# A fused cross-attention, Fourier mixing and MLP kernel: another order of the calls of its opening

## The chip, the cores and the metric

The kernel runs on one core of a Trainium2 chip. The metric is the device time of one execution in microseconds; a kernel's time is the median of several executions. Five engines work side by side, each through its own instructions in order: PE (TensorE, matrix products and transposes), DVE (VectorE), ACT (ScalarE), POOL (GpSimd) and SP (SyncE, which here only issues transfers). PE's results go into PSUM, a small memory in banks, from which DVE and ACT fetch them. Transfers to and from DRAM are issued by SP, ACT and POOL and are carried out by 16 DMA engines. Engines wait for each other by semaphores.

## The reference

For each of 8 batches there are two attentions, of the tokens `x` over the state and of the state over the tokens. Both results are set one below the other (512 + 32 = 544 rows of 8 heads x 64 = 512 columns). On this the real part of a two-dimensional Fourier transform is added, the rows are normed, and a two-layer perceptron is added.

```python
# x (8, 8, 512, 64), state (8, 8, 32, 64), float32
a = softmax(x @ state.T / 8);   xread = a @ state
a2 = softmax(state @ x.T / 8);  sread = a2 @ x
x = concatenate([xread, sread], axis=2)        # to (8, 544, 512)
u = x + real(fft(fft(x, axis=1), axis=2))
un = (u - mean(u)) / sqrt(var(u) + 1e-6)       # over the last axis
out = u + relu(un @ w_ch1) @ w_ch2             # 512 -> 2048 -> 512
```

## The kernel before

**How it is staged.** The batches run through a pipeline: while the perceptron of batch b keeps PE busy (`layer1`: products `ph`, ACT's `hT`; `layer2`: `po`, `poA`, `poB`), the attention of batch b+2 and the transform of batch b+1 are woven in. Tokens and state are cast to bf16 (`xin`, `stb`), transposed (`xT`, `sT`), multiplied to scores (`esp`), passed through the exponential on ACT, and multiplied by the state (`xrp`). DVE divides by the sums and writes the reads forwards and backwards as `XF` and `XR`. The transform along the 544 rows uses sums and differences of mirrored rows and columns (`Sm`, `SS`), multiplied by cosines and sines `TC`, `TS` and their negatives `NN` into `gp`; it is copied to `G` and multiplied by the second axis's table `TEO` into `yp`. `U` is the sum with x, `ub` its centred bf16 form, `tp` the transpose of `ub` on PE and `unT` its copy for `layer1`.

**The opening.** Before the first `ph` (at 22.4 us) nothing of the pipeline is full. `load_x(0)` fetches batch 0's tokens in seven pieces (four of 96 or 128 rows, then 15, 15 and 2 rows), two through ACT's queue and the rest through SP's, with `load_state(0, 1)` first on SP. `load_state(1, 2)` and `load_x(1)` do so for batch 1, all on SP. `turn_in_dram` copies a state mirrored from DRAM to DRAM (`s_dram`), and a later `load_state(..., s_dram)` reads it back into `gen`. `state_blocks(lo, hi, copy)` makes four casts into `stb`, one for each 32 partitions; batch 0's are ACT's, later ones POOL's. `cast_x` casts one piece of x to `xin`: for batch 0 one on ACT and three on DVE, for batch 1 on POOL. The sine tables come from counts: POOL's `iota` writes, DVE's `turn_steps` and `low_arguments` reduce them to angles in `gen`, and POOL's four `tensor_scalar` on `gi` make the second axis's angles. ACT evaluates them with its sine table and must load a table when it goes between sine and exponential; tiny activations on `gate2` (rows `gate` in the profile) stand where the load is to happen. `first_weights(lo, hi)` and `second_weights` issue the quarters of `w1` and `w2` on POOL, 512 KB each. `open_batch` holds batch 0's attention (`turn`, `score`, `read`, `sread`, `state_rows`, `even`, `odd`). `make_mirror` sets up `mirror` by a memset and an affine select on POOL; PE's `eTp` of batch 1 uses it. `warm(n)` issues n small products of `blank` whose results nobody uses.

**What sets the order.** All calls on the engines go through a `Recorder`, which stores them as 1748 numbered groups: one call each, except that consecutive products into the same PSUM bank, and batch 0's first loads, form one. At the end `play()` makes the calls in the order of the list `ORDER`. The text after it keeps that order on each engine; the waits between engines are derived from the data. So one call ahead of another of its engine in `ORDER` is ahead of it on the chip, and a call that waits holds up all that stand behind it on its engine. [...] `BANKS["psB"]` gives the bank, one digit for each tile of the pool `psB` in order of request; a tile waits for its bank's previous tile to be read out.

Because of the recorder every row in the profile carries line 63, where the stored call is made; rows are told apart by tile names and shapes. In the file, `ORDER` stands at line 68, `BANKS` at 133, `load_state` at 256, `load_x` at 265, `state_blocks` at 311, `low_arguments` at 404, `first_weights` at 459, `open_batch` at 718 and `warm` at 1269. The recorder's play and the gate that opens the sine table read:

```python
    def play(self):
        order = ORDER or range(len(self.groups))
        for n in order:
            for call in self.groups[n][1]:
                made = call()
...
    nc.vector.memset(gate2, 0.0)
    nc.scalar.activation(gate2[:, 1:2], gate2[:, 0:1], AF.Sin)
    state_ones(0, 2)
    state_blocks(0, 1)
    cast_x(0, nc.scalar.copy, 2, 3)
```

Of the kernel before, what the change touches and what calls it, by code (L numbers as in the profile page):

```python
# [49 lines left out]
class _Engine:  # L50
# [3 lines left out]
    def __getattr__(self, what):  # L54
# [14 lines left out]
        19 62 66 61 9-10 12 1 7 11 2 5 4 3 163 8 49 13 6 298 14 55 15 17 16 50 22 0 75-82 29 143 25 27 26 47 28 38 31 41 23  # L69
        144-145 40 39 32 146-147 30 20 46 21 42 48 148 43-45 149 18 24 34-35 33 37 36 72-74 83-118 130 119 329 120-121 123 122  # L70
        155 131 157 124 156 168 330 172 125 141 170 126 169 171 173 142 176 127-129 133-134 184 178 180 192 68 54 159 69-71 177
        185 193 59-60 58 67 64 316 63 65 187 189 186 135-137 188 138 194 196 195 197 139-140 153-154 216 174 331-332 175 206-210
        212 179 211 181 221 219 213 222 132 150-151 182 152 190 198-199 191 217 214 218 200 263 160 167 201-202 51 265 161
        203-204 267-268 165-166 205 299 162 56 261-262 300 158 264 304 266 297 307 303 302 301 57 228 232 229 220 225-227 224
        233 245 223 244 241 183 215 236-240 252-254 231 235 234 230 276-277 247-248 278-279 246 250-251 259 257 255 269 256 272
        249 242-243 258 271 274 284 270 273 317 312 310 309 319 315 314 313 311 318 280-283 285 290 292-293 291 294 275 286 288
        323 322 287 327 326 320 289 321 328 343 324 341 325 345 339 347 340 348 355 333 337 353 378 351 335 386 354 352 346 387
        361 360 342 338 344 385 379 362-365 367 308 260 366 368 52 296 358 382 381 398 356 390-391 380 383-384 521 392-393 396
        394 439 401 400 399 336 357 359 397 334 402-404 406 405 408 407 409 522 413-414 505 523-524 410 415 412 411 441 525 305
        371 370 369 373 422 374 419 375 426 424 420 423 53 526 421 417-418 459 457 349 376 455 453 461 476 465 388 463 473 469  # L80
        467 460 395 350 440 462 456 454 377 458 464 470 468 466 389 472 488 474 480 518 451 481 445-446 449 482 450 487 484 491
        442 492 447 485 496 475 477-478 443 448 495 500-501 506 429-430 428 427 452 591 493 486 479 483 529 536 497 516 498 489
        517 502 499 490 578 164 306 579 507 503 574 527 504 471 508 372 576 580 528 575 416 577 433 432 435 437 434 431 436 543
        582 512 532 519 530 494 583 514 444 520 531 550 533 539 537 589 509 540 538 560-563 510 555 544 556 545 511 438 546 549
        772 547 553 548 559 552 557 554 584 558 598 592 534 585-586 630 622 600 564 569 567 601 606 614 587-588 593 602-603 573
        568 572 570-571 607-608 596 595 597 594 609-610 621 611 613 612 616-617 625 618 627 626 620 619 604 541 624 632 637 599
        535 551 631 615 605 590 623 638 542 652 677 633 641 639 635 565 634 642 640 636 646 661 668 628 566 653 662 678 647 649
        671 654 648 655 670 663 669 664 684 689 685 690 680 682 650 644 659 672 629 683 658 681 667 651 688 693 645 673 660
        714-715 751 704 736-737 757 761 716-717 701 656 700 740 699 295 698 718 728 727 729 657 730 733 732 731 581 674-675
        694-695 679 767 762 782 708 774-775 768 922 745 744 705 771 742 769 741 746 743 738 752 739 754 756 706 763-764 758 755  # L90
        753 776-777 709 778 783 779-780 791 786 790 794-795 787 789 788 702-703 676 713 796 697 765 818 812 864 784 792 802 797
        804 816 814 871 759 808 719 820 766 813 865 819 793 803 785 798 815 805 817 760 809 821 830 823 711 725 720 710 825 726
        712 707 722 806 810 873 799 828 734 880 837 723 721 826 824 827 735 800 781 801 747-748 849 862 842 831 872 807 874 829
        881 836 835 846 850 838 840 839 841 811 863 845 843 852 870 724 773 770 851 750 844 866 858 856 875 911 832 893 877 884
        882 892 833 883 876 857 696 853 859 867 887-888 919 904 886 902 907 974 908 889-890 912 903 921 665-666 891 822 896 691
        847 895 848 899 898 897 900-901 692 686 643 687 954 932 914 878 909-910 920 894 955 928-929 934 968 834 960 957 959 925
        923-924 879 1102 941-942 970 980 996 963 917 976 905 1035 991 987 939 969 975 997 1046 981 933 906 1036 964 918 992 940
        930 913 931 935 943 916 915 937 944-948 938 971 965 949 966 986 950 977 988 967 953 952 951 978 984 993 1103 927 936 958
        973 926 962 961 956 1047 989 982 1007 985 994 979 990 983 1008 1048 1003 998 1012 1040 1009 1053 1022 1024 1058 1101
        1000 999 1001 1014 1005 1013 1004 1002 1041 1006 1054 1010 1025 1011 1060 1086 1061 1051 1067 1077-1078 1049 1062  # L100
        1015-1016 1063 1023 1059 1018 1027 1052 1064 1070 868 1071 1073-1074 1072 860 869 861 854 1075-1076 855 1079-1080 1050
        1087 1140 1017 1026 1031 1042 1280 1105 1104 1107 515 1134 1139 1137-1138 1106 1082 1037 1097-1098 1055 1119 1146 1084
        1236 1112 1069 1065 1056 1083 1099-1100 1066 1088 1038 1091 1113 1132 1108 1148 1094 1213 1166 1164 1110 1120 1019 1028
        1147 1237 1133 1114 1089-1090 1115-1116 1118 1117 1126 1122 1095 1081 1121 1124 1123 1141 1096 1143 1142 1130 1125 1111
        1144 1158 1205 1154 1092 1193 1162 1168 1127 1160 1149 1032 1085 1214 1165 1043 1109 1159 1167 1155 1206 1093 1194 1169
        1145 1131 1128 1161 1163 1174 1231 1207 1188 1219 1150 1175-1177 1151 1178 1057 1039 1136 1135 513 1179 1232 1220
        1181-1182 1180 1279 995 1020-1021 425 1029 1238-1239 1183 1172 1225 1156 1264 1191 1229 1226 1157 1192 1230 1185 1208
        1173 1171 1186 1189 1240 1184 1241 1190 1187 1243 1201 1196 1224 1197 1281-1282 1129 1068 1153 1200 1285 1195 1283-1284
        1209 1215 1255 1245 1256 1260 1227 1288 1257-1258 1244 1228 1247 1274 1261 1198 1030 1242 1044 1248 1250 1254 1249 1170
        1253 1199 1045 1033-1034 1275-1276 1221 1233 1335 1272 1277 1222 1289 1259 1265 1304 1273 1278 1308 1268 1305 1270  # L110
        1290-1291 1315 1252 1251 1267 1316 1292 1266 1234 1286 1321 1331 1297 1364 1343 1319 1327 1337 1376 1310 1407 1262 1293
        1269 1294 1296 1306 1295 1322 1312 1314 1332 1344 1299 1313 1300 1303 1301 1309 1342 1361 1302 1271 1202 1210 1287 1336
        1298 1320 1328 1216 1377 1365 1395 1408 1311 1338 1333 1325 1339 1359 1329 1340 1334 1326 1330 1317 1354 1402 1390 1360
        1318 1391 1403 1263 1398 1378 1435 1409-1410 1345 1357 1356 1355 1358 1379 1411 1399 1412 1348 1346-1347 1349 1367 1372
        1352 1368 1353 1307 1323 1235 1223 1386 1380 1366 1371 1413 1419 1421 1211-1212 1420 1217 1424-1425 1203-1204 1218 1341
        1423 1422 1369-1370 1392 1404 1426-1427 1416 1400 1362 1446-1447 1396 1384 1350 1428 1436 1429 1440 1393 1405 1363 1373
        1397 1351 1385 1401 1454-1455 1481 1491 1431 1441 1474 1461 1536 1450 1492 1482 1475 1462 1451 1439 1438 1418 1448-1449
        1456-1457 1468 1437 1458 1460 1459 1463 1476 1478 1464 1414-1415 1432 1445 1465-1466 1452 1512 1570 1499 1501 1489 1443
        1453 1477 1467 1444 1430 1497 1493 1469 1479 1537 1442 1513 1500 1490 1502 1498 1494 1472 1470 1473 1480 1516 1483 1507
        1495 1485 1524 1563 1519 1517-1518 1496 1520 1486 1508 1510 1509 1504 1511 1394 1406 1521 1505 1433 1538 1484 1527 1381  # L120
        1532 1525 1514 1564 1387 1528 1434 1515 1506 1523 1539 1522 1544 1554 1567 1558 1556 1550 1557 1540 1546 1471 1526 1531
# [1433 lines left out]
```

## Time and profile before

| what | value |
|---|---|
| time, median of three runs | 287.75 us (287.4 to 288.25) |
| profiled execution, its own time | 287.47 us |
| its span, from first to last instruction | 285.7 us |
| mean granted clock of PE | 0.997 |
| instructions | 6835 |
| PE busy in 0 to 10 us / 10 to 20 / 20 to 30 | 7.02 / 9.95 / 9.53 us |
| first product of `layer1` (`ph`) | 22.39 us |
| DMA engines' mean busy share of the span, first and second slice of 7.14 us | over 80%, over 90% |

The profiled execution's time is 1.77 us longer than its span: the span leaves out what lies around the instructions. In rows of the timeline the columns are start, duration, engine, line, operation, tiles, shapes and number of instructions, and in brackets the idle time of the engine before them with what ended it. `x4` after a row means that four instructions follow each other in it. Of a chain the columns are start, duration and what it consisted of. The page's slices:

```profile
PE   7899999999999999999999999999999999999993
DVE  6877777468899988985798688959766578224892
ACT  7897656746936576368377564586566653254000
POOL 8392476670660033502712119006200028000000
DMA  8999959966366346861379640413201520978366
```

Each digit is a tenth of a slice's time for which the engine was busy. PE is below nine tenths in the first two slices and the last one only.

### The profile page before, as it was taken

The page shows a single profiled execution, that of the slowest core. Times are in us where ns is not written, and L with a number is a line of the kernel's source. Part 1 is how long each engine was busy: PE and PEld are TensorE (multiplying, and loading weights), DVE is VectorE, ACT ScalarE, POOL GpSimd, SP SyncE. Part 2 cuts the span into 40 slices and gives each one's busy share as a digit, 9 for nine tenths or more (in the row PEclk, how much of TensorE's full clock was granted, in tenths as well). Part 3 has the DMA queues.
Part 4 walks back from the last instruction along what each step waited for, and adds up shares of the span by engine and source line. Part 5 has one row for each costly group of instructions (what it writes and reads, how often), then busy time and mean ns, then how long its engine had stood idle before and what let it go on. Part 6 is the DMA issues. An engine that isn't in the chain of part 4 may idle for free.

```text
span 285.7 us, 6835 instructions
## 1 busy us (share of the span) xinstructions
PE 275.2 (96%) x2615; PEld 199.0 (70%) x2644; DVE 210.6 (74%) x554; ACT 162.0 (57%) x327; POOL 92.5 (32%) x227
## 2 busy tenths in 40 slices
PE   7899999999999999999999999999999999999993
PEld 6788985555655778567758777576577667686882
DVE  6877777468899988985798688959766578224892
ACT  7897656746936576368377564586566653254000
POOL 8392476670660033502712119006200028000000
PEclk9999999999999999999999999999999999999998
DMA  8999959966366346861379640413201520978366
GB/s 156 185 181 190 202 95 181 197 146 153 83 157 103 93 116 156 107 170 25 80 169 194 149 94 19 98 53 65 84 0 48 151 65 18 182 149 136 92 162 184
DMA packets 110972, 34.91 MB, mean 122 GB/s; under 512 B 101996, under 2 KB 106476, under 8 KB 110940
## 3 DMA queue, kind: packets, MB, share of 16 engines
q1 hardware_dynamic: 100220, 28.72, 47.5%
q0 software_dynamic: 4224, 4.19, 9.7%
q10 hardware_dynamic: 6496, 1.57, 2.6%
q8 instruction: 20, 0.33, 0.5%
q14 instruction: 12, 0.10, 0.1%
HBM read 22.41 MB, written 14.02 MB: 128 GB/s over the span
## 4 chain that ended last, share of the span: by engine, by line
PE 87%; DVE 7%; DMA 2%; issue 1%; ACT 1%; SPq 1%; DVEq 0%
PE ph L63 39%; PE poA L63 18%; PE poB L63 13%; PE gp L63 4%; PE po L63 3%; PE yp L63 2%; DVE U L63 2%; DMA xs<-in_x_dram 2%; PE esp L63 2%; PE eTp L63 1%; PE xrp L63 1%; DVE XR L63 1%; PE xfp L63 1%; DVE ot L63 1%; SPq L63 1%
## 5 line engine op out<-in xcount | busy, mean ns | idle before, releaser
L63 PE MATMUL ph<-unT,w 128*128 128x512 bf16 (+2 forms) x743 | 127.9, 315 | 1.4
L63 ACT ACTIVATE hT<-ph 128x512 bf16<-128x512 f32 x128 | 72.1, 596 | 76.6 <-PE ph L63 76.3
L63 PEld LDWEIGHTS <-w 128*128 128x128 bf16 x768 | 64.3, 98 | 42.5 <-issue 0.6
L63 PEld LDWEIGHTS <-hT 128*128 128x128 bf16 x632 | 60.4, 98 | 14.8 <-issue 0.3
L63 DVE SCALAR_TENSOR_TENSOR ot<-poA,rstd,U 128x256 f32<-128x256 f32 (+1 forms) x46 | 21.7, 475 | 16.5 <-PE poA L63 13.8
L63 POOL CAST xin<-xs 128x2048 bf16<-128x2048 f32 (+3 forms) x14 | 14.5, 1046 | 48.5 <-PE poA L63 20.3
L63 PE MATMUL poB<-w,hT 128*128 128x256 bf16 x224 | 28.2, 273 | 0.0
L63 POOL TENSOR_TENSOR rstd<-rstd,mhalf 128x1 f32<-128x1 f32 x34 | 20.3, 604 | 1.1
L63 POOL TENSOR_TENSOR rstd<-mv,epst 128x1 f32<-128x1 f32 x14 | 2.8, 211 | 42.9 <-DVE mv L63 42.9
L63 ACT CAST G<-gp 128x288 bf16<-128x288 f32 (+2 forms) x31 | 12.8, 477 | 5.6 <-PE gp L63 5.3
L63 ACT ACTIVATE ub<-U,S 128x512 bf16<-128x512 f32 (+1 forms) x22 | 15.1, 706 | 1.5 <-DVE U L63 1.3
L63 PE MATMUL po<-w,hT 128*128 128x512 bf16 x60 | 15.4, 379 | 0.2
L63 PE MATMUL poB<-TA,SA 128*128 128x256 bf16 x120 | 15.5, 273 | 0.1
L63 PE MATMUL poA<-TA,SB 128*128 128x256 bf16 x120 | 15.6, 273 | 0.0
L63 DVE SCALAR_TENSOR_TENSOR U<-yp,XF 128x2 f32<-128x2 f32 (+1 forms) x24 | 10.0, 419 | 7.5 <-PE yp L63 5.3
L63 DVE SCALAR_TENSOR_TENSOR ot<-poB,rstd,ot 128x256 f32<-128x256 f32 x30 | 14.2, 478 | 1.0 <-PE poB L63 0.8
L63 PE MATMUL poA<-TC,hT 128*128 128x256 bf16 (+1 forms) x120 | 14.5, 265 | 0.1
L63 POOL COPY XT<-XR 32x514 bf16<-32x514 bf16 x7 | 4.2, 605 | 31.8 <-DVE U L63 15.8
L63 PE MATMUL poA<-w,hT 128*128 128x256 bf16 x112 | 14.5, 273 | 0.0
L63 ACT ACTIVATE junk<-U,S 128x512 bf16<-128x512 f32 x20 | 14.3, 716 | 0.2
L63 PE MATMUL poA<-TB,hT 128*128 128x256 bf16 x112 | 14.3, 273 | 0.0
L63 DVE SCALAR_TENSOR_TENSOR ot<-poB,rstd,U 128x256 f32<-128x256 f32 x15 | 7.2, 478 | 9.0 <-PE poB L63 9.0
(197 smaller groups left out, 478.3 us busy)
## 6 DMA issues: line engine op xcount, KB each, us to landing
xs<-in_x_dram SPq DMA_DIRECT2D x22, 256.0 KB, 3.8
w<-in_moe_w_ch_dram POOLq DMA_DIRECT2D x8, 512.0 KB, 6.8
out_dram<-ot SPq DMA_DIRECT2D x15, 256.0 KB, 2.4
r_dram<-ot SPq DMA_DIRECT2D x14, 256.0 KB, 2.4
out_dram<-r_dram SPq DMA_DIRECT2D x14, 256.0 KB, 3.7
xs<-in_x_dram SPq DMA_DIRECT2D x8, 192.0 KB, 4.9
xs<-in_x_dram ACTq DMA_DIRECT2D x2, 256.0 KB, 4.7
l_dram<-ot SPq DMA_DIRECT2D x2, 256.0 KB, 2.0
```

Source lines behind the costliest of these rows:

```text
L63: self._rec.add(self._name, lambda: f(*args, **kw), key)
```

## The change

Two literals are replaced; no function, tile, size or call changes. `ORDER` holds the same 1748 numbers. From its 438th place on they are the same in both versions; 403 of the first 437 places hold another number. `BANKS["psB"]` gives other banks to nearly all tiles from the seventh on, to the kernel's end. On the engines the following comes of it:

- **SP:** after batch 0's loads stands `load_state(1, 2)` (before: behind the six of the first loads, four x pieces and one mirror copy of batch 1). Then come batch 1's x pieces, smaller ones before the last two large ones, then the mirror copies and their reads, with a transpose by DMA of batch 2's state between them.
- **DVE:** the memset of `gate2` stands behind the casts `pf`, the low rows' arguments and their first counts. The memset of `blank` stands earlier. `XF` of piece 0 is divided before `XR` of piece 3. The `tensor_scalar` of the second table comes behind the four divisions.
- **ACT:** the gate that opens the sine table (which reads `gate2`) stands ahead of the four `stb` casts and the cast of `xin`'s piece 2. One `NN<-TC` negation stands before the table load for the exponentials. The last table load stands behind `ub` and the copy of `xT`.
- **POOL:** one quarter of `w1` (the first) is issued ahead of the low rows' work; the other three come behind the copies and casts for batch 0's low rows and around batch 1's x casts, and in another sequence (0, 2, 1, 3 instead of 2, 0, 1, 3). Batch 1's four `stb` casts stand ahead of the copy `XB<-XR`. One cast of a batch 1 x piece stands before these weights. The affine select of `mirror` stands behind an `stb` cast of batch 2's state.
- **PE:** the 144 products of `warm` are dealt out otherwise: 31 instead of 44 before the first transpose of x, more between the reads. Batch 1's state transposes come before `low_of`, whose parts are in another sequence. The first `ph` takes the quarters of `w1` in the new order, and `srp` stands behind `xrp`.

```diff
--- before
+++ after
 ORDER = [i for p in """
-        19 62 66 61 9-10 12 1 7 11 2 5 4 3 163 8 49 13 6 298 14 55 15 17 16 50 22 0 75-82 29 143 25 27 26 47 28 38 31 41 23
-        144-145 40 39 32 146-147 30 20 46 21 42 48 148 43-45 149 18 24 34-35 33 37 36 72-74 83-118 130 119 329 120-121 123 122
-        155 131 157 124 156 168 330 172 125 141 170 126 169 171 173 142 176 127-129 133-134 184 178 180 192 68 54 159 69-71 177
-        185 193 59-60 58 67 64 316 63 65 187 189 186 135-137 188 138 194 196 195 197 139-140 153-154 216 174 331-332 175 206-210
-        212 179 211 181 221 219 213 222 132 150-151 182 152 190 198-199 191 217 214 218 200 263 160 167 201-202 51 265 161
-        203-204 267-268 165-166 205 299 162 56 261-262 300 158 264 304 266 297 307 303 302 301 57 228 232 229 220 225-227 224
...
+        19 58 60 64 62 65 63 9 4 8 7 11 16 10 12 3 17 1-2 5 14 160 13 49 299 50 15 6 20 0 22 25 143 38 29 144-146 47 41 147
+        31-32 27 39-40 30 42 21 23 26 43 28 44 148 45-46 149 75-87 18 24 36-37 33-35 72-73 223 74 88-105 130 106-123 131 150 155
+        157 124 156 329-330 168 331-332 172 125 141 170 169 171 151 173 142 126-127 176 128-129 133-134 184 192 68 54 51 163 165
+        69 268 55 70 159 266 71 265 267 177 185 193 61 59 66-67 186 188 187 189 135-140 178 180 194 196 195 153-154 197 174-175
+        206-209 216 211 210 212-213 221 294 179 181 219 152 48 190-191 198 182 199 217 200 214 218 215 183 132 201 203-204 202
+        298 264 167 166 52 263 261 57 297 262 301 205 300 162 307-308 302-303 296 304 228 232 220 229 225-227 244 233 245 224
...
 """.split() for i in range(int(p.split("-")[0]), int(p.split("-")[-1]) + 1)]
 BANKS = {
     "psB":
-        "042530035243124510132233540105502155414354505141402034405101533004110553420510442332502451515042303354055545304330535010"
-        "450505431422351534114200530023121414424400541351510051314313231504211132145515551253042352444441503512220533144155040455"
-        "32003553050321355351104231340210145150040533005150435"
+        "042530413250523014211544310530204321024310124505024230021525133220552113042152004334124015151204323310211101320332131252"
+        "012121035044315130550422132243545050040022105315152215350353435120455534501151115413204314000005123154442133500511202011"
+        "34223113212345311315520435302452501512202133221512031"
```

## The prediction

> **What bounds the kernel now.** I read the page first: engine shares and the chain that ended last.
>
> ```profile
> PE 275.2 (96%) x2615; PEld 199.0 (70%) x2644; DVE 210.6 (74%) x554; ACT 162.0 (57%) x327; POOL 92.5 (32%) x227
> PE 87%; DVE 7%; DMA 2%; issue 1%; ACT 1%; SPq 1%; DVEq 0%
> ```
>
> TensorE is busy 96% and 87% of the chain. The diff leaves every call in place from the 438th number on, so it can shift only the opening, up to the first `ph` at 22.39 us and some 15 us after it. That stage I read in the chain over 0 to 45 us, the timelines of ACT, POOL, PE, and the waits over 0 to 24 us.
>
> ```profile
> 3.60 4.75 DMA xs<-in_x_dram
> 8.46 0.44 DVE xin L63
> 10.06 0.78 PE esp L63 x22
> 12.09 0.70 DVE XR L63
> 13.83 0.70 PE warm L63 x6
> 16.84 2.53 PE gp L63 x29
> 21.99 0.36 DVE unT L63
> 22.39 1.05 PE ph L63 x16
> ```
>
> Here (start, duration, what) the opening is a relay, not one engine: batch 0's last large load lands at 8.35, then cast, scores, reads, DVE's divisions, the transform on PE, `unT`, `ph`. A delay on any engine of the relay reaches `ph`.
>
> ```profile
> 3.20 0.20 ACT L63 ACTIVATE gate<-gate 128x1 f32<-128x1 f32 x1
> 8.24 0.59 ACT L63 COPY xT<-xTp 128x512 bf16<-128x512 bf16 x1 [0.43 <-PE xTp L63]
> 9.81 1.75 ACT L63 ACTIVATE EE<-esp 128x512 bf16<-128x512 f32 x3 [0.48 <-PE esp L63]
> 13.74 0.43 ACT L63 ACTIVATE NN<-TS 128x288 bf16<-128x288 bf16 x1
> 14.84 0.60 ACT L63 CAST XR<-warm 32x512 bf16<-32x512 f32 x1 [0.67 <-POOL XB L63]
> 14.34 0.28 POOL L63 CAST stb<-gen 32x128 bf16<-32x128 f32 x1 [0.60 <-DMA gen<-in_state_dram]
> 15.48 0.69 DVE L63 TENSOR_TENSOR Sm<-XF,XR 128x1028 bf16<-128x1028 bf16 x1 [0.31 <-ACT XR L63]
> 28.40 0.40 PE L63 MATMUL xfp<-stb,ET 128*128 128x260 bf16 x2 [0.21 <-DVE XR L63]
> ```
>
> Brackets give idle time and its releaser. Two waits stand out: POOL idles 0.60 on batch 1's state, ACT then 0.67 behind POOL; but ACT has only 0.43 + 0.48 idle before the exponentials.
>
> **Step 1: batch 1's state earlier (expected gain).** On SP it goes from place 13 to place 7, ahead of batch 1's x. It was issued at 9.24 and used at 14.34; now it is issued near 4.4, behind the load at 3.60, and at that load's 4.75 us lands by 9.2. Removed: the 0.60 and what follows of the 0.67. The four `stb` casts (0.28 to 0.31 each) move to about 11 to 12.5, before the `XB` copy (12.93 before). They delay that copy to some 13.6 to 14.2 if `XR0` is later too, which takes most of the gain back, but `XR`'s wait is on the bits behind the copy and these no longer wait for a load. Price of the removal: up to -0.67 on `Sm`, if nothing else is late.
>
> **Step 2: `gate2` memset late (expected loss).** In DVE's built order this memset (2.84, 0.06 us) falls behind the `pf` casts, which wait for POOL's iotas, the low rows' arguments and the first counts (the 288-wide scalar row at 4.08 takes 0.36). Adding those rows puts it at 4.7 to 5.0. ACT's sine-table gate needs it, and now stands ahead of the `stb` copies and the cast of `xin` piece 2. So the gate goes from 3.20 to 4.75 to 5.05. From gate to second table end ACT runs without idle: 7.81 - 3.20 = 4.6; one `NN<-TC` of 0.4 (two took 0.76 at 15.69) is moved in front of the table load: 5.0. Batch 0's `xT` copy thus starts at 9.75 to 10.05 instead of 8.24. Waiting 0.43 and 0.48 absorbs part: copy and four `EE` without idle take 0.49 + 3 x 0.49 + 0.60 = 2.56 (starts lie 0.49 apart), so the last `EE` ends at 12.3 to 12.6; it was 11.56. That is +0.75 to +1.0. Behind it table load and sines take 2.27 (11.57 to 13.84), ending 14.6 to 14.9; `XR` was at 14.84 only through its 0.67 wait, so it starts at 14.95 to 15.25 and `Sm` at 15.6 to 15.9: **+0.1 to +0.4**. `low_of` (14.50) starts +0.1 to +0.45 late, as it needs `TC`'s second half. Step 1's gain is thus the cover that ACT's loss uses up; without step 1 the loss would be the whole 0.75 to 1.0.
>
> **Step 3: casts of batch 1 and what PE waits for.** POOL casts one x piece earlier (about 15 instead of 18.19) and finishes at 19.5 to 19.95 (20.29 before). PE waited 0.19 for it at 20.35. That frees 0 to 0.19 of PE time, but `ph` then waits on `unT`, so I count 0. ACT's table load of 1.28 at 19.53 goes behind `xT`: its `ub` ended at 21.42, 0.24 after DVE's. I count -0.1, since `tp` at 21.48 would still need DVE's. Sum at `ph`: +0.14 to +0.45, less 0.1: +0.04 to +0.35.
>
> **Step 4: after `ph`.** `srp` is put behind `xrp` and fills PE while DVE makes `XR` (27.65, 0.71); the idle 0.37 before 28.40 (of it 0.21 put down to `XR`) goes. On the other side `tp` and `xrp` there now follow sooner on `ub` and `ET`, which I price at 0.1 to 0.3 by their lateness in step 3. Net -0.27 to -0.07. DVE's reordered divisions (`XF` of piece 0 ahead of `XR` of piece 3, 0.70 each) fill a wait and cost nothing unless `XB` waits for `XR`: then 0.70 on POOL's copy, whose 0.38 idle is the cover.
>
> **Step 5: weights.** The first `w1` quarter is triggered near 7.4 (before: 11.59), the others near 15.6 to 17.7 (before from 15.48).
>
> ```profile
> 11.59 0.96 POOL L63 DMA_DIRECT2D w<-in_moe_w_ch_dram  x1
> 15.48 2.31 POOL L63 DMA_DIRECT2D w<-in_moe_w_ch_dram  x3
> 19.31 0.29 POOL L63 TENSOR_SCALAR_AFFINE_SELECT mirror<-mirror 128x128 bf16<-128x128 bf16 x1
> w<-in_moe_w_ch_dram POOLq DMA_DIRECT2D x8, 512.0 KB, 6.8
> ```
>
> At a median 6.8 us three quarters land by 24.5, used at 22.39 on; the order of use is turned to quarter 0, 2, 1 accordingly: quarter 2 landed 17.5 before and would by 15.6 + 6.8 = 22.4 now, against a use at about 23.8. Cost 0, cover 1.4. The early quarter shares the load time with batch 1's x. Lower bound 0 (x is cast from 15 on), upper +1: batch 1 has 1.06 MB, and over 6 to 14 us the core moved about 200 GB/s, so 0.5 MB more is 2.5 us against landings at 11.8 to 14.7 and uses at 15 to 19. I take 0, nearer to the uses. [...]
>
> **Step 6: PE's fillers.** With `xin` piece 2 cast at about 6.0 and only 31 fillers before it, PE idles from about 4.3 to 6.0 (before no gap until 5.9).
>
> ```profile
> 3.00:3.50 0.50, 0.50 (x7) 0.00 (x0) 0.00 (x0) 1.00 1.28 287
> 4.50:5.00 0.50, 0.50 (x13) 0.00 (x0) 0.00 (x0) 1.00 1.29 208
> ```
>
> This view counts the fillers in windows of 0.5 us (in brackets; the 1.00 is the granted clock): seven or eight fit early, thirteen later, while the granted clock reads 1.00 in both: the pitch falls by almost half near 4.2 us. If the idle keeps the slow pitch through 7.6 to 11, PE's 2.0 us of work there doubles, partly in waits: 0 to +1.2. I take 0, as the row at 7.81 shows quick work after a 0.88 idle. [...]
>
> **Sum.** +0.04 to +0.35 at `ph`, -0.27 to -0.07 after it, 0 for weights and clock: -0.2 to +0.3. Its middle is +0.05. Steps 5 and 6 were counted at 0 but can only lose (0 to +1.0 and 0 to +1.2), so I add a quarter of the smaller, +0.25: **+0.3**. The profiled execution becomes 287.47 + 0.3 = 287.8; it is 0.28 under the median, so the median becomes 288.05. Own range 287.5 to 288.6.
>
> **Rivals.** (a) Faster: `gate2` is not late, and the removed idles all count: -0.67, -0.19, -0.37, -0.1 = -1.3, 286.4. For: the waits are in the profile. Against: the relay had several other limits within 0.3 us. Chance 0.22. (b) Slower, mirror: `mirror`'s affine select now stands on POOL behind an `stb` copy that waits for the mirrored state of batch 2, read back from DRAM. That load is issued about 15.5 on SP and takes 4.2 us (10.29 to 14.49) up to 7.7 (29.45 to 37.11, beside weights): 19.7 to 23.2, then 0.3 + 0.8 + 0.3. PE's `eTp` wants it at 24.9, so it decides from a landing after 23.5; price +1 to +1.5, 289.0. Chance 0.12. (c) Slower, clock or x (steps 5, 6): +1.0, 288.75. Chance 0.12. (d) ACT's 0.75 to 1.0 reaches `ph` entire, without step 1's cover, and step 4 gives nothing: 288.65; chance 0.09. (e) Nothing: the stages hide all; 287.75, inside the forecast.
>
> **Numbers.** Forecast with (e) 0.45. Below 0.3% (0.86 us) a difference can't be told from no change here. Faster 0.22; same 0.45; slower 0.33, which is (b), (c) and (d) together. The 80% range reaches to (a)'s and (b)'s centres: 286.5 to 289.4.
>
> **What would show it.** Right: `gate` at 4.7 to 5.0, `EE` ending at 12.3 or later, no 0.60 wait of POOL `stb`, `Sm` at 15.6 to 15.9, `ph` at 22.4 to 22.8, no wait of `xfp` on `XR`. Wrong: `gate` before 4, `ph` before 22 or after 23, `eTp` waiting for `mirror`, filler pitch slow after 7 us.

## The result, and the profile after

The changed kernel takes 290.73 us in the median of five executions, the kernel before 287.71: a ratio of 1.0094, 95% interval 1.0075 to 1.0113. It is slower by 3 us, outside both ranges of the prediction (287.5 to 288.6, and 286.5 to 289.4 for 80%). One of the five took 298.35 us; experiment 7 shows a stall of that size in other orders.

The page's first part and the chain's shares hardly differ from those before; DVE is busy 3.4 us longer with the same instructions:

```profile
span 288.6 us, 6836 instructions
PE 277.4 (96%) x2615; PEld 200.9 (70%) x2644; DVE 214.0 (74%) x554; ACT 162.4 (56%) x327; POOL 92.2 (32%) x227
PE 86%; DVE 8%; issue 2%; ACT 1%; POOL 1%; POOLq 0%; DVEq 0%
```

The chain of the changed kernel over 0 to 60 us (start, duration, what) says where the time went:

```profile
4.44 0.37 DVE gen L63
5.42 0.63 ACT xin L63
6.71 2.45 PE warm L63 x23
11.46 0.76 PE esp L63 x22
13.59 0.70 DVE XR L63
...
17.07 1.10 DVE Sm L63
18.19 1.41 DVE SS L63 x3
...
25.30 1.05 PE ph L63 x16
```

`ph` starts at 25.30, before at 22.39: +2.91, and the whole span grows by 2.9. From `ph` to the end both profiled executions take 263.3 us. So the loss lies in the opening, where the two orders differ (the last place of `ORDER` with another number is the 438th), and nothing is won or lost behind it. The head of the chain is another than before: it was the load that lands at 8.35; now it is DVE's counts, ACT's cast of `xin`, and 23 of PE's fillers, work that nobody needs. Further on `Sm` and `SS` on DVE stand in it. ACT's timeline:

```profile
4.88 0.20 ACT L63 ACTIVATE gate<-gate 128x1 f32<-128x1 f32 x1 [1.69 <-DVE stb L63]
10.11 0.59 ACT L63 COPY xT<-xTp 128x512 bf16<-128x512 bf16 x1 [0.36 <-PE xTp L63]
10.59 2.38 ACT L63 ACTIVATE EE<-esp 128x512 bf16<-128x512 f32 x4
16.34 0.60 ACT L63 CAST XR<-warm 32x512 bf16<-32x512 f32 x1 [0.61 <-PE warm L63]
```

The gate is 1.68 late and waits for DVE; the exponentials start 0.59 apart in the mean, without a wait that the profile shows, and end at 12.97, 1.40 later than before (11.57). Note that `xT`'s copy waits for PE, not for ACT's own table load. PE before, then PE, DVE and POOL after, the last three in the same execution:

```profile
1.53 3.91 PE L63 MATMUL warm<-blank 128*128 128x128 bf16 x44 [1.53 <-DVE blank L63]
5.28 0.39 PE L63 MATMUL xTp<-ident,xin 128*128 128x128 bf16 x4
```

```profile
1.01 3.49 PE L63 MATMUL warm<-blank 128*128 128x128 bf16 x31 [1.01 <-DVE blank L63]
6.10 0.61 PE L63 MATMUL xTp<-ident,xin 128*128 128x128 bf16 x4 [1.60 <-ACT xin L63]
6.50 2.02 PE L63 MATMUL warm<-blank 128*128 128x128 bf16 x17
```

```profile
17.07 1.09 DVE L63 TENSOR_TENSOR Sm<-XF,XR 128x1028 bf16<-128x1028 bf16 x1
18.19 1.20 DVE L63 TENSOR_TENSOR SS<-Sm 128x256 bf16<-128x256 bf16 x2
19.51 0.59 DVE L63 TENSOR_TENSOR NN<-Sm 128x2 bf16<-128x2 bf16 x1
20.02 0.84 DVE L63 TENSOR_TENSOR SS<-Sm 128x512 bf16<-128x512 bf16 x2
```

```profile
16.10 1.57 POOL L63 DMA_DIRECT2D w<-in_moe_w_ch_dram  x2
17.69 1.54 POOL L63 CAST xin<-xs 128x512 bf16<-128x512 f32 x2
```

PE idles 1.60 for the cast, and then starts its 17 fillers 0.107 apart (the row behind them starts at 8.32): the slow pitch of its first 31 (0.106 apart, from 1.01 to 4.18), where pitch is the time from one product's start to the next. On DVE `Sm` takes 1.09 instead of 0.69 and the first two rows of `SS` 1.20 instead of 0.50; POOL casts beside them. DVE's rows before:

```profile
16.21 0.50 DVE L63 TENSOR_TENSOR SS<-Sm 128x256 bf16<-128x256 bf16 x2
16.76 0.76 DVE L63 TENSOR_TENSOR SS<-Sm 128x512 bf16<-128x512 bf16 x2
```

From the start of `Sm` to the end of the last `SS` row made from it pass 3.79 us; before it was 2.04.

The 2.91 us in stretches, each read from the two timelines:

| stretch | before | after | difference |
|---|---|---|---|
| start to the last `EE`'s end | 11.57 | 12.97 | +1.40 |
| from there to `Sm` | 3.91 | 4.10 | +0.19 |
| `Sm` to `SS` made | 2.04 | 3.79 | +1.75 |
| from there to `ph` | 4.87 | 4.44 | -0.43 |

What the -0.43 is made of was not tested.

### The profile page after: what moved, and what is told of

It reads as the page before. It is cut to its first block, busy times and chain, and to the rows that moved or that the text cites. A ratio compares the mean times of both kernels' runs of the same rounds, so it can differ in the third digit from the quotient of the medians.

```text
span 288.6 us, 6836 instructions
## 1 busy us (share of the span) xinstructions
PE 277.4 (96%) x2615; PEld 200.9 (70%) x2644; DVE 214.0 (74%) x554; ACT 162.4 (56%) x327; POOL 92.2 (32%) x227
## 4 chain that ended last, share of the span: by engine, by line
PE 86%; DVE 8%; issue 2%; ACT 1%; POOL 1%; POOLq 0%; DVEq 0%
PE ph L63 39%; PE poA L63 17%; PE poB L63 13%; PE po L63 3%; PE gp L63 3%; PE yp L63 2%; DVE U L63 2%; PE esp L63 2%; PE warm L63 1%; PE xrp L63 1%; PE eTp L63 1%; DVE XR L63 1%; DVE ot L63 1%; PE xfp L63 1%; PE srp L63 1%
## 5 line engine op out<-in xcount | busy, mean ns | idle before, releaser
L63 DVE SCALAR_TENSOR_TENSOR U<-yp,XF 128x510 f32<-128x510 f32 (+1 forms) x24 | 10.0, 418 | 7.5 <-PE yp L63 5.3
```

Source lines behind the costliest of these rows:

```text
L63: self._rec.add(self._name, lambda: f(*args, **kw), key)
```

## The experiments

Names with a_ are the changed kernel with an edit, names with b_ the kernel before with one. The edits move numbers in `ORDER` and change nothing else. Ratios are against the kernel before, on the same chip. `EE` end, `Sm`, "stretch" (start of `Sm` to `SS` made) and `ph` are of each run's one profiled execution.

**1. The gate put back (a_gate).** 23 is `gate2`'s memset.

```diff
-20 0 22 25
+20 0 23 22 25
-42 21 23 26
+42 21 26
```

> The changed kernel with one call moved: DVE's memset of gate2 back to the second place on DVE. Theory G (the late gate makes ACT late, and that carries on to Sm): gate at 3.1 to 3.3 instead of 4.88, last EE ends at 11.8 to 12.3 instead of 12.97, Sm starts 0.7 to 1.1 earlier than 17.07, total 289.6 to 290.1. Theory C (the other half is POOL's casts of batch 1 beside Sm and SS): from Sm's start to SS's end still 3.2 to 3.8 us. If the late gate were the only cause (theory N), that stretch would fall to about 2.0 and the total to about 288.

Measured: gate 3.20, last `EE` end 11.63, `Sm` 15.72, stretch 3.62, `ph` 23.95; and yet 297.88 us, ratio 1.0333 (1.0299 to 1.0367). In the opening this has G's direction and C's stretch: 1.35 earlier at `Sm` and at `ph`, the stretch hardly shorter. It is more than G gave (0.7 to 1.1, `EE` to end at 11.8 or later); in this execution PE's idle is 1.03 instead of 1.60, and its pitch turned quick at 3.9, ahead of the idle. The total is neither theory's. PE idles near 51 us, which experiment 7 takes up.

**2. POOL's casts put behind triggers (a_casts), and both moves (a_gate_casts).**

```diff
-264 167 166 52 263 261 57 297 262 301 205 300 162 307-308 302-303
+167 166 205 307-308 52 264 263 261 57 297 262 301 300 162 302-303
```

> The changed kernel with POOL's four casts of batch 1's x put behind five weight triggers instead of among them (the last w1 quarter and the first two of w2 go ahead of them). Theory C: Sm takes 0.69 instead of 1.09, Sm's start to SS's end 2.0 to 2.5 instead of 3.79, total 289.0 to 289.5. Theory N (the DVE rows are long for another reason, such as weights landing in SBUF): 3.5 or more, total 290.5 to 290.9; more weights are then in flight in that stretch than before, so it could even grow.

> Both moves at once. If G and C are two separate causes the gains add: Sm's start 0.7 to 1.1 earlier and Sm's start to SS's end 2.0 to 2.5, total 287.8 to 288.7. If they are one, no better than the better one of the two alone.

Measured: a_casts 289.73 us, ratio 1.0065 (1.0052 to 1.0079), stretch 3.57; a_gate_casts 289.45 us, 1.0055 (1.0037 to 1.0073), stretch 3.57, `Sm` 15.59, `ph` 23.60: G's gain is there again, C's is in neither. C as I had put it fell: without a cast beside them the first two `SS` rows are as long as before. DVE's and POOL's timelines of a_casts:

```profile
16.89 0.69 DVE L63 TENSOR_TENSOR Sm<-XF,XR 128x1028 bf16<-128x1028 bf16 x1
17.62 1.20 DVE L63 TENSOR_TENSOR SS<-Sm 128x256 bf16<-128x256 bf16 x2
18.74 0.65 DVE L63 COPY SS<-Sm 128x2 bf16<-128x2 bf16 x1
```

```profile
15.47 3.92 POOL L63 DMA_DIRECT2D w<-in_moe_w_ch_dram  x5
19.36 0.15 POOL L63 MEMSET epst<- 128x1 f32 x1
19.40 2.09 POOL L63 CAST xin<-xs 128x512 bf16<-128x512 f32 x3
```

POOL was never free in that time either: triggers stood in the place of the casts. The copy `SS<-Sm` ends at 19.39, with the last trigger. So the theory became C2: a running POOL row holds DVE's row until it ends. In this breadth the kernel before speaks against it: three triggers run there from 15.48 to 17.79, and the two `SS` rows beside them take 0.50.

**3. POOL held while `SS` is made (a_idle).** 260 is POOL's tiny row `gate<-SS`, which waits for `SS`.

```diff
-298 264 167 166 52 263 261 57 297 262 301 205 300 162 307-308 302-303 296 304 228
+298 228
-253 252 254 231
+253 252 254 260 264 167 166 52 263 261 57 297 262 301 205 300 162 307-308 302-303 296 304 231
```

> The changed kernel with POOL held: its row gate<-SS (which waits for SS) goes ahead of batch 1's x casts and the weight triggers, so that POOL does nothing while DVE makes Sm and SS. Theory C2 (any running POOL row, cast or trigger, holds DVE's bf16 rows until it ends): Sm's start to SS's end falls from 3.79 to 1.7 to 2.0, with no row of SS over 0.45. Theory N (ACT's, PE's or the transfers' work stretches SS): it stays above 3. The total is no test: casts and weights come 3 us later, so ph can wait for w1, 289 to 294.

DVE's timeline:

```profile
16.90 0.70 DVE L63 TENSOR_TENSOR Sm<-XF,XR 128x1028 bf16<-128x1028 bf16 x1
17.63 0.50 DVE L63 TENSOR_TENSOR SS<-Sm 128x256 bf16<-128x256 bf16 x2
18.11 0.16 DVE L63 TENSOR_TENSOR NN<-Sm 128x2 bf16<-128x2 bf16 x1
18.19 0.76 DVE L63 TENSOR_TENSOR SS<-Sm 128x512 bf16<-128x512 bf16 x2
```

With POOL idle the rows are 0.70, 0.50, 0.16, 0.76 and the stretch 2.04 instead of 3.79, a little over the 1.7 to 2.0 of C2. ACT and PE keep the changed kernel's order, so they are not what stretches `SS`, and N fell for them. The transfers are not the same: from 17 to 19 us the core moves 22 and 0 GB/s, in the changed kernel 78 and 101. Against them as the cause stands the kernel before, whose two `SS` rows take 0.50 in a microsecond with 206 GB/s (16 to 17). (Total 296.15 us, 1.0262, 1.0225 to 1.03: casts and weights come too late, and by more than the 289 to 294 expected.)

**4. The collision put into the kernel before (b_casts).** Two casts of batch 1's x go ahead of three weight triggers.

```diff
-267-268 165-166 205 299 162 56 261-262 300
+267-268 261-262 165-166 205 299 162 56 300
```

> The kernel before with two of POOL's casts of batch 1's x moved ahead of the three weight triggers at 15.48, into the time of Sm and SS on DVE. Theory C: Sm and SS stretch, Sm's start to SS's end 2.7 to 3.3 instead of 2.04, total +0.6 to +1.3 (288.3 to 289.0). Theory N: that stretch stays near 2.0 and the total within 0.3 of the kernel before.

Measured: 288.14 us, ratio 1.001 (0.9998 to 1.0022), stretch 2.74, `ph` 23.16. Its timelines:

```profile
16.43 1.20 DVE L63 TENSOR_TENSOR SS<-Sm 128x256 bf16<-128x256 bf16 x2
```

```profile
15.81 1.68 POOL L63 CAST xin<-xs 128x512 bf16<-128x512 f32 x2
```

The casts take 1.68 instead of 1.17 beside `Sm` (0.69, untouched), then the two `SS` rows 1.20 instead of 0.50. Taken singly, the casts end at 16.87 and 17.49 and the `SS` rows at 17.01 and 17.63, each 0.14 after a cast. Here no trigger runs until 17.44, so casts alone do it, and the rows of both engines are longer for it. `ph` is 0.77 later and the total about 0.5 us longer, just under the 288.3 to 289.0 that C gave; the interval just reaches 1.

**5. The gate alone (b_gate), the fillers alone (b_fill), both (b_gate_fill), and in the changed kernel the fillers put back (a_fill).** In b_gate one `NN<-TC` (223) also stands before the table load, as in the change.

```diff
-31 41 23 144-145
+31 41 144-145
-43-45 149
+43 23 44-45 149
-72-74 83-118
+72-73 223 74 83-118
-233 245 223 244
+233 245 244
```

b_fill, and b_gate_fill on top of b_gate:

```diff
-83-118 130 119
+83-105 130 106-118 119
```

a_fill:

```diff
-88-105 130 106-123
+88-118 130 119-123
```

> The kernel before with the gate of the change alone: gate2's memset behind DVE's first counts and rests, and one NN<-TC on ACT ahead of the table load. Gate at 4.7 to 5.0 instead of 3.20. As the prediction's step 2 has it, xT's copy starts at 9.75 to 10.1, the last EE ends at 12.3 to 12.6, Sm starts 0.1 to 0.5 late, total +0.1 to +0.5 (287.8 to 288.3). Theory G as read from the changed kernel: Sm starts 1.0 to 1.6 late, total 288.7 to 289.3.

> The kernel before with 13 of the 44 fillers moved behind the first transposes of x, and the gate left early (the other half of b_gate_fill). Theory K as a sum of two parts: the fillers alone cost what b_gate_fill cost above b_gate, +1.0 to +1.6 (288.7 to 289.3), with PE's pitch slow until 8 us. Theory K as a product (it takes the late cast as well, since x's piece is cast at 5.0 here and PE hardly idles): pitch quick from 5 us on, the last EE at 11.3 to 11.9, total within 0.4 of the kernel before.

> The kernel before with the change's gate (as in b_gate) and, besides, 13 of the 44 fillers moved behind the first transposes of x, as in the change. Theory K (late cast and few fillers together let PE idle, and its pitch falls back): PE idles from about 4.9 to 6.0, filler pitch near 0.107 until 8.5, last EE ends 0.5 to 0.9 later than in b_gate (12.11), total 0.5 to 1.0 above b_gate (288.6 to 289.2). Against K: the last EE within 0.2 of 12.11 and the total within 0.3 of b_gate.

> The changed kernel with 13 of PE's fillers moved from behind the first transposes of x to ahead of them, so that 44 stand there as before and PE does not idle from 4.50 to 6.10. Theory K (PE's slow pitch after that idle makes transposes and EE late): filler pitch 0.055 instead of 0.107 from 6.5 on, xTp of the second to fourth piece up to 1 us earlier, last EE ends at 12.2 to 12.6, total 290.1 to 290.5. Theory G (ACT alone is late): xT's copy still waits for ACT's table load until 9.75, the last EE ends at 12.6 or later, total 290.4 to 290.8.

| run | us | ratio (interval) | `EE` end | `Sm` | `ph` |
|---|---|---|---|---|---|
| b_gate | 288.11 | 1.001 (0.9996 to 1.0023) | 12.11 | 15.87 | 22.76 |
| b_fill | 287.58 | 0.9997 (0.9981 to 1.0012) | 11.63 | 15.34 | 22.45 |
| b_gate_fill | 289.54 | 1.0057 (1.0035 to 1.0079) | 13.58 | 17.16 | 24.43 |
| a_fill | 298.15 | 1.0336 (1.0312 to 1.036) | 12.17 | 16.29 | 24.11 |

The late gate alone makes `ph` 0.37 late and the total about 0.4 us longer (the interval just reaches 1), the fillers alone nothing that can be seen, both together 1.9 us. That is more than K gave (288.6 to 289.2, with `EE` 0.5 to 0.9 later than in b_gate; it is 1.47 later), but it has K's sign: a product of the two, not a sum. Experiment 6 measures the pair again. In a_fill the gate is as late as in the changed kernel (4.88), but `EE` ends 0.80 and `ph` 1.19 earlier; its PE has 44 fillers before the transposes and 0.40 us of idle (of the 1.19, 0.42 are a shorter stretch, 3.37):

```profile
6.10 0.40 PE L63 MATMUL xTp<-ident,xin 128*128 128x128 bf16 x4 [0.40 <-ACT xin L63]
6.34 0.39 PE L63 MATMUL warm<-blank 128*128 128x128 bf16 x4
```

From 6.10 on PE runs at the quick pitch, where the changed kernel runs slow until about 9.8. a_fill's total has the same late stall as a_gate.

**6. Does the idle always delay the quick pitch? (b_all, and the changed kernel and b_gate_fill again.)** b_all is b_gate_fill with the move of b_casts.

> The kernel before with the three parts put in: late gate and 13 fillers moved (b_gate_fill, +1.9 over before) and two casts of batch 1's x ahead of the weight triggers (b_casts, +0.5). If they add: 289.8 to 290.3, ph at 24.8 to 25.4. If the casts only fill time that PE's lateness leaves, as b_gate_fill: 289.3 to 289.7.

> The changed kernel unaltered, on one chip beside b_gate_fill. In its profile PE idled 1.9 us before 6.1 and its quick pitch came at 9.4 or later. Theory W (whether an idle of that size delays the quick pitch depends on where it falls in time, which differs between executions): most executions at 290.3 to 291.0, now and then one 1 to 1.5 lower. Theory K (the idle always delays it): all within 290.4 to 291.0, apart from those with the late stall (296 or more).

> The kernel before with late gate and 13 fillers moved, again, since b_all, which has the same idle, had the quick pitch at 6.5 and 288.45. Theory W: executions in two groups, near 288.0 (quick pitch at 6.5) and near 289.5 (at 8.6 or later). Theory K: all near 289.5.

(The 1.9 us of idle in the second of these count from the start of the last filler, 4.18; the profile's idle is 1.60.)

b_all took 288.45 us, ratio 1.0027 (1.0017 to 1.0038): far under the 289.8 to 290.3 expected, although it has the same 1.53 of idle; its twelve executions lie between 288.05 and 289.32. PE of b_gate_fill, then of b_all:

```profile
6.55 0.61 PE L63 MATMUL xTp<-ident,xin 128*128 128x128 bf16 x4 [1.53 <-ACT xin L63]
6.96 2.02 PE L63 MATMUL warm<-blank 128*128 128x128 bf16 x17
```

```profile
6.54 0.40 PE L63 MATMUL xTp<-ident,xin 128*128 128x128 bf16 x4 [1.53 <-ACT xin L63]
6.77 1.11 PE L63 MATMUL warm<-blank 128*128 128x128 bf16 x17
```

The order is the same on PE, the idle is the same, and in one execution PE comes out of it slow, in the other quick. b_gate_fill again: nine executions, two at 287.88 and 287.93, seven between 288.99 and 289.63 (ratio 1.0038, 1.0022 to 1.0054; 1.25 us over the kernel before, where the first run had 1.9). The changed kernel again: 289.41 to 290.83, 289.99 in the median (1.0079, 1.0063 to 1.0095), spread without two clear groups. b_gate_fill's times fall into W's two groups, in its first run too (one at 287.87, five from 289.02 to 290.30). Both of its profiles are of slow ones (quick pitch at 10.8 and 9.6), so that its quick executions are those with the early quick pitch is inferred from b_all. For the changed kernel W's groups are not to be seen, but K's narrow band isn't either.

**7. The stall near 51 us (a_gate_mirror), and all three causes taken out (a_all).** POOL's timeline of a_gate, then PE's:

```profile
23.90 0.29 POOL L63 CAST stb<-gen 32x128 bf16<-32x128 f32 x1 [5.53 <-DMA gen<-s_dram]
24.36 0.75 POOL L63 DMA_DIRECT2D w<-in_moe_w_ch_dram  x1 [0.18 <-issue]
...
51.46 0.61 POOL L63 CAST xin<-xs 128x508 bf16<-128x508 f32 x1 [8.78 <-DMA xs<-in_x_dram]
```

```profile
56.66 1.22 PE L63 MATMUL tp<-ident,ub 128*128 128x128 bf16 x8 [5.57 <-ACT ub L63]
```

POOL waits 5.53 for batch 2's mirrored state. SP had issued the read back at 16.88, behind two `w1` triggers at 14.75 and 15.58; in the changed kernel it is issued at 16.28, together with them, and there the cast runs at 20.03 without a wait. The weights that stand behind the waiting cast are triggered at 24.4 to 27.1 instead of 20.5 to 23.1. SP's reads for the later batches slip too, and the last large piece of batch 2's x, issued at 42.05 beside the `w2` triggers of 40.86 and 41.94, takes 9.26 us; in the changed kernel it is issued at 40.87, ahead of these triggers (42.19 and 43.27). From `ph` to the end a_gate takes 271.7 us instead of 263.3. So in a_gate a quicker opening, in which the weights come earlier and the read back does not, is followed by a stall of 8 us. a_fill's profile has the same (waits of 4.37 for the mirrored state and 8.91 for x). In a_gate_casts the cast waits too (2.86), but the weights stand ahead of it, and none of six executions is over 290.66.

a_gate_mirror, on top of a_gate, moves the mirror copy (66) and the read back (67):

```diff
-19 58 60 64
+19 58 60 66-67 64
-59 66-67 186
+59 186
```

a_all, on top of a_gate, changes POOL's order:

```diff
-201 203-204 202 298 264 167 166 52 263 261 57 297 262 301 205 300 162 307-308 302-303 296 304 228
+298 201 203-204 202 264 167 166 228
-253 252 254 231
+253 252 254 260 52 263 261 57 297 262 205 300 162 307-308 301-303 296 304 231
```

> a_gate (the changed kernel with the early gate2 memset), with the mirror copy of batch 2's state and its read back moved on SP from behind batch 1's x to behind its first piece. Theory S (a_gate's stall of 6 us near 51 comes from the late read back: POOL's stb cast waits for it, the weights behind it come late, SP's loads of batch 2's x slip into the transfer of w2): POOL's wait goes, the last w1 quarter is triggered before 19, batch 2's x is cast before 46, no stall, total 288.8 to 289.6. Against S: the stall stays, 296 to 299.

> The changed kernel with all three suspected causes taken out: gate2's memset early; POOL held from the second weight trigger until SS is made, by its row gate<-SS; and the weights and mirror set ahead of the stb cast that waits for batch 2's state. If gate with idle PE, POOL beside SS, and the late read back are the whole loss: Sm at 15.5 to 15.8, Sm's start to SS's end near 2.04, ph at 22.0 to 22.5, no stall near 51, total 287.2 to 288.0. If something of the new order is left that these do not name: 288.5 or more.

a_gate_mirror: POOL's wait is gone, batch 2's x is cast from 42.98 on, five of six executions show 289.2 to 290.7 and one 297.17; ratio 1.0082 (1.0066 to 1.0097), stretch 4.18. The median, 290.19, lies above what was expected, and the last `w1` quarter is triggered at 20.50, not before 19: POOL now waits 1.43 for batch 1's x, which stands behind the mirror copy. a_all: 287.88 us, ratio 1.0011 (0.9992 to 1.003); `Sm` 15.58, stretch 2.04, `ph` 22.50. Apart from POOL's order everything else of the change is still in it, the banks too. The late gate with the idle PE, and POOL beside `SS`, are the whole loss of the changed kernel against the kernel before, as far as a ratio with this interval can tell; the late read back was followed by the stall in the profiles of a_gate and a_fill, whose openings are quicker, and not in the changed kernel's. Two of a_all's twelve executions took over 296.5, so the late stall is not wholly out of the order, and what brings it on in single executions was not profiled.

**8. What the change had to give (b_state, b_best).** In b_state the load of batch 1's state (58) moves; b_best also has `srp` (378) behind `xrp`.

```diff
-19 62 66 61
+19 58 62 66 61
-59-60 58 67
+59-60 67
```

b_best, on top of b_state:

```diff
-353 378 351 335
+353 351 335
-361 360 342
+361 360 378 342
```

> The kernel before with load_state of batch 1 alone moved to SP's first place behind batch 0's loads, as in the change. POOL's 0.60 wait for it goes, and of ACT's 0.67 wait for XB as much as XR is next in line: Sm starts up to 0.5 earlier. Prediction's step 1: -0.3 to -0.6 (287.1 to 287.4). Rival: batch 1's x pieces land later and take it back, 287.5 to 288.0.

> The kernel before with two single moves of the change: batch 1's state first on SP (b_state) and srp behind xrp on PE. If srp covers the 0.37 gap before xfp, 0.2 to 0.4 under b_state: 286.9 to 287.2. If something else ends last there, as b_state: 287.2 to 287.5.

POOL's and ACT's timelines of b_state:

```profile
13.48 0.28 POOL L63 CAST stb<-gen 32x128 bf16<-32x128 f32 x1
```

```profile
14.17 0.60 ACT L63 CAST XR<-warm 32x512 bf16<-32x512 f32 x1 [0.24 <-POOL XB L63]
```

POOL's 0.60 wait is gone, ACT's is 0.24 instead of 0.67, `Sm` starts at 14.81 and `ph` at 21.87: 287.3 us, ratio 0.9982 (0.9969 to 0.9996), which just leaves out 1. b_best is not better: 287.61 us, 1.0008 (0.9993 to 1.0024). Its gap before `xfp` is gone, but from `ph` to the end it takes 263.24 us, against 263.36 in b_state. Up to `ph` the two have the same order, and ACT's wait is 0.24 in both; yet b_best has `EE` end at 11.73 and `Sm` at 15.21, b_state 11.33 and 14.81. The rest of b_state's gain is thus batch 0's x, cast earlier in that execution (last cast on DVE at 8.23, in b_best at 8.63, before at 8.46). These two profiles of one opening differ by 0.4 to 0.5 us, so a difference as small as b_gate's in a single profile proves little.

The banks of `psB` were not tried apart from the order; a_all has the new ones.

## Why the prediction was wrong

**Step 1** had the wait right: POOL's 0.60 goes, and of ACT's 0.67 there go 0.43 (b_state and b_best). That b_state shows -0.67 at `Sm`, the figure named, is luck, as 0.24 of it is x that came earlier; b_best shows -0.27. In the changed kernel the gain does not arrive: ACT's `XR` waits 0.61 for PE's `warm` there instead of for POOL (the row at 16.34), and 0.61 in a_all too.

**Step 2** had the late gate right (4.88; 4.75 to 5.05 said), though the gate stands ahead of the `stb` and `xin` casts in the kernel before too (3.20 and 3.41); new is only its late memset. Alone (b_gate) it ends `EE` at 12.11, not 12.3 to 12.6, and makes `Sm` 0.39 late. The step gave +0.1 to +0.4 with step 1's cover and 0.75 to 1.0 without it; b_gate has no such cover, so the cover was not needed. In the changed kernel `EE` ends at 12.97, and `XR` starts at 16.34 instead of 14.95 to 15.25: the transposes that ACT's copy waits for were late on PE, and the exponentials start 0.59 apart in the mean, where the step took 0.49. (The sum at `ph` begins with +0.14 to +0.45, which no row gives; the step has +0.1 to +0.4.)

**Step 6 is the first that failed.** It saw the idle (4.3 to 6.0 said, 4.50 to 6.10 measured) and counted it at 0, "as the row at 7.81 shows quick work after a 0.88 idle". That row comes from a time when PE had been running quick from near 4.2 to 6.93; here its 31 fillers were still 0.106 apart when the idle began at 4.50. In eleven profiled executions of these kernels with at most 1.3 us from the start of the last filler to that of the first transpose, the quick pitch came between 3.9 (a_gate) and 7.0; in six of seven with 1.8 to 1.9 us it came between 9.3 and 10.8 (b_gate_fill; the changed kernel 9.8), in the seventh (b_all) at 6.5. The price, 0.80 at `EE` and 0.78 at `Sm` (a_fill), lies inside the 0 to +1.2 that step 6 had and then counted at 0 (a quarter, +0.25, was added for steps 5 and 6 together). It was part of a rival with a chance of 0.12, and these runs make it the usual case. I let the row decide, though it did not answer the same question.

**Step 3 is the second.** It had POOL's casts of batch 1's x begin at about 15 us and end by 19.95 (15.54 and 20.07 measured) and priced them on PE alone, 0 to -0.19. Who else runs in that time was not asked: `Sm` and `SS` on DVE, which take 3.79 instead of 2.04. The missing term is +1.75, the largest of all, and no rival had it. In b_casts the first two `SS` rows take 1.20 beside casts alone and end 0.14 after them, and the casts take 1.68 instead of 1.17. In a_casts and a_gate_casts the same rows take 1.20 beside triggers only; in the kernel before they take 0.50 beside triggers. What decides between those two was not found.

**Step 4** saw the gap before `xfp` go, but from `ph` to the end nothing changed: 263.30 and 263.29, where -0.27 to -0.07 was said.

**Step 5** was right for the first `ph`: no wait for `w1`, and x in time. **Rival (b)** named the wait of the `stb` cast for the mirrored state, and that it might come at 23.2. In the changed kernel it is just not reached (20.03); in a_gate it is (23.90), and its price is not 1 to 1.5 us on `eTp` but 8 us nearly thirty microseconds later, at the loads of batch 2.

## What to carry to other kernels

When a row is moved in time, look up what the other engines do at its new place, not only who waits for it: POOL's casts and DVE's `SS` rows both took longer beside each other here (1.68 instead of 1.17 and 1.20 instead of 0.50 in b_casts), and the waits tables show nothing of it, only durations that have grown. Dealing out PE's fillers differently can change when its pitch turns quick (by 6.94 in b_gate and 5.10 in b_fill, at 10.8 and 9.6 in b_gate_fill's two profiles): a late cast and fewer fillers, which alone cost 0.4 us or nothing that can be seen, cost 1.3 and 1.9 us together in two runs. A big reordering is best tried one move at a time: of the moves tried singly none cost more than 0.5 us and one may have gained 0.4, and the whole cost 3.

## What was not expected of the hardware

The granted clock reads 1.00 in every window of the first ten microseconds, while the fillers start 0.107 us apart in some (the changed kernel's 17 from 6.50) and 0.055 in others (four from 5.50 in the kernel before); the pitch has to be read from the counts of instructions. When it turns quick differs between executions of one and the same order: 10.8 and 9.6 in b_gate_fill's two profiles, and 6.5 in b_all, whose order on PE is the same. Nine executions of b_gate_fill fall into 287.9 and 289.0 to 289.6. What sets the moment was not found. And a load of 256 KB of x took 9.26 us in a_gate beside two weight triggers; the median of such loads over the whole changed kernel is 3.5.
